# Decode step of attention and a gated MLP: the hidden vector as five neighbours a partition, w_out as the stationary operand

## The chip, the cores and the metric

The kernel runs on one core of a Trainium2 chip. The metric is the device time of one execution in microseconds; three runs of the kernel before gave 286.37, 286.49 and 287.57, with a median of 286.49. The profile is of a further execution, of 285.96 us, whose recorded span is 284.3 us. All times below inside the kernel count from the start of that span.

## What is computed

One token passes through one layer. The token x has D = 640 values. First, attention over the last 4096 keys of a cache of 32 heads with 192 values each; then a gated MLP of width 768. Cut to what matters:

```
q      = layernorm(x) @ wq                       # 640 -> 32 heads x 192
p      = softmax(q . k * 192**-0.5)              # over the last 4096 keys of each head
h      = x + (p . v) @ wo                        # 6144 -> 640
z      = gelu(layernorm(h) @ w_in)               # 640 -> 1536, halves z1 and z2
g      = w_sp * layernorm(z2) + b_sp             # one position: w_sp and b_sp are scalars
out    = h + (z1 * g) @ w_out                    # 768 -> 640, bf16
```

Nearly all bytes are keys and values: the page counts 119.34 MB read from memory.

## The kernel before

The work is a stream. All large loads go through one queue of SyncE in a fixed order, the list `plan`: wq, then keys `k_t` and values `v_t` of a pair of heads in turn (16 pairs), an eighth of wo (`wo_t`) after every second pair, and last the four pieces of w_in and the six of w_out. A load is issued when a buffer of its pool is free (`issue` and `free`): six for keys and values, two for wo. The schedule is written by hand (`manual_schedule`): each engine executes its instructions in the order in which the program text emits them.

For each pair, VectorE multiplies keys by the query (line 320), TensorE and ScalarE or VectorE add up the products (327, 310, 313), softmax follows with a maximum and `exps`, and TensorE multiplies by the values (`values`, 406 and 416). `scaled` and `columns`/`columns2` bring the result of a pair of pairs into columns, and `project` multiplies it by its eighth of wo:

- For the first seven eighths the result `o` is the stationary operand, one column wide, and rows of wo move. The sums lie in `rows`, a part of the PSUM bank `attn_ps`, in partitions 0 and 32 for the output columns up to `CUT[1]` = 384, and in 64 and 96 for the other 256 (line 477). x is added there as well (471).
- Then ScalarE copies `rows` to `rows_sb` (558), and `fold` (491) turns the rows into columns of `attn_ps` with three fp32 matmuls, each of 128 columns of `rows_sb` as the stationary operand against `halfsel`, which adds partitions 0 and 32, or 64 and 96. TensorE executes an fp32 matmul as two passes, so the profile shows six.
- For the last eighth a block of 128 columns of wo is the stationary operand and `o` moves (482), accumulating into the same columns. Its load comes in two halves, and each half of the projection has 15 matmuls.

So h lies in `attn_ps` as five columns of 128 partitions: value c x 128 + p in partition p, column c. From here on there is no more parallel work. Line 578 copies h to `h_pc` with its sum, 580 squares it, two matmuls with a matrix of 1/640 (582, 584) give the mean and mean square in every partition, and `ln_rstd16` (232 to 239) works out the reciprocal root on VectorE in five small instructions. `half_in` (593) does 30 matmuls with blocks of w_in as the stationary operand, first for z2, later for z1. After gelu (599), the second layernorm takes its sums by line 601 and the matmul 613; `gz` (622) is the gate, z1's gelu is line 625, and `gv` (627) their product.

The output of the MLP is formed as rows again. `orow` is a PSUM bank with four groups of 160 values, in partitions 0, 32, 64 and 96. `h_rows` writes h into it by 16 passes of fp32 matmuls against an identity, one half of them ahead of the matmul of line 613 and one half behind it. Then 24 matmuls with one column of `gv` as the stationary operand and 160 columns of w_out moving (630) add the MLP's output. VectorE casts the bank to bf16 (633), and the store writes four rows of 320 bytes (634).

Of the kernel before, what the change touches and what calls it, by code (L numbers as in the profile page):

```python
# [8 lines left out]
BF16 = mybir.dt.bfloat16  # L9
F32 = mybir.dt.float32  # L10
I32 = mybir.dt.int32
ALU = mybir.AluOpType
ACT = mybir.ActivationFunctionType
AX = mybir.AxisListType

@with_exitstack
def kernel(
# [14 lines left out]
    nc = tc.nc  # L32
    P = nc.NUM_PARTITIONS
    _, H, Sk, Dh = A_k_cache.shape
    D = A_x.shape[-1]
# [3 lines left out]
    DC = D // P  # L39
# [4 lines left out]
    FHC = Fh // P  # L44
# [23 lines left out]
    RQ = 4 * Dh // P  # L68
    NQ = NP // 2
    wo_v = A_wo.rearrange("(q e i) n -> q e (i n)", q=NQ, e=NE16)  # L70
    win_v = B_w_in.rearrange("(c p) f -> p c f", p=P)
    wout_v = B_w_out.rearrange("(c e i) n -> c e (i n)", c=FHC, e=NE16)
    wq_v = A_wq.rearrange("(c p i) n -> c p (i n)", c=DC, i=4)
    LAST = (0, J // 2, 3 * J // 4, 7 * J // 8, J)
# [8 lines left out]
    const = ctx.enter_context(tc.tile_pool(name="const", bufs=1))  # L83
    small = ctx.enter_context(tc.tile_pool(name="small", bufs=3))
    psum = ctx.enter_context(tc.tile_pool(name="psum", bufs=2, space=bass.MemoryType.PSUM))

    def sc_bank():
        return psum.tile([P, 512], F32, tag="sc", name="sc_ps", bufs=2)

    def bank():  # L90
        return psum.tile([P, 512], F32, tag="sm", name="sm_ps", bufs=3)
# [7 lines left out]
    w_out_sb = wp.tile([P, FHC, D], BF16)  # L99
# [51 lines left out]
    def free(kind, n=1):  # L151
        live[kind] -= n
        issue()
# [21 lines left out]
    ident_f = const.tile([P, P], F32)  # L175
# [8 lines left out]
    for a in range(2):  # L184
        nc.vector.tensor_reduce(out=par[:, a:a + 1], in_=ident_f[:].rearrange("p (g a s) -> p a g s", a=2, s=2)[:, a],
                                axis=AX.XY, op=ALU.add)
# [22 lines left out]
            nc.vector.tensor_reduce(out=blocks[:, h_, k_:k_ + 1], in_=id_h[:, c0:c0 + 2, :], axis=AX.XY, op=ALU.add)  # L209
    m8 = const.tile([P, 8], F32)  # L210
    nc.vector.tensor_tensor(out=m8[:], in0=blocks[:, 0, :], in1=blocks[:, 1, :], op=ALU.add)
    halfsel = const.tile([P, 2], F32)
    for h_ in range(2):
        nc.vector.tensor_reduce(out=halfsel[:, h_:h_ + 1], in_=ident_f[:, 64 * h_:64 * h_ + 64:32], axis=AX.X, op=ALU.add)
    pv_tiles = []
    for i in range(2):
        pv_tiles.append(psum.tile([P, 512], F32, name=f"pv{i}", bufs=1))
# [7 lines left out]
    def neg_var(mean, square):  # L225
        v = small.tile([P, 1], F32, tag="lnv", name="lnv")
        nc.vector.tensor_scalar(out=v[:], in0=mean, scalar1=mean, scalar2=square, op0=ALU.mult, op1=ALU.subtract)
        return v
# [25 lines left out]
    for a in range(2):  # L254
        nc.vector.tensor_scalar(out=xn2[:, :, a, :].rearrange("p c (g a s) -> p c a g s", a=2, s=2)[:, :, a],
                                in0=x_pc[:, 0, 0:DC, None, None].to_broadcast([P, DC, HALF // 2, 2]),
# [5 lines left out]
    for gq in range(0, NQ, 4):  # L262
        for w0 in range(0, 2 * Dh, P):
            psv = sc_bank()[:].rearrange("p (q w) -> p q w", q=4)
            for c in range(DC):
                wc = wq_sb[c // 2][:, (c % 2) * HD:(c % 2 + 1) * HD].rearrange("p (q a w) -> p q a w", q=NQ, a=2)
                for a in range(2):
                    nc.tensor.matmul(psv, lhsT=xn2[:, c, a, :], rhs=wc[:, gq:gq + 4, a, w0:w0 + P],  # L268
                                     start=(c == 0 and a == 0), stop=(c == DC - 1 and a == 1))
# [7 lines left out]
        nc.vector.tensor_scalar(out=sp_f[:, k_:k_ + 1], in0=sp_ps[:, c_:c_ + 1], scalar1=w_, scalar2=None, op0=ALU.mult)  # L277

    attn_ps = psum.tile([P, 512], F32, tag="acc", name="attn_ps", bufs=1)
    CUT = (0, 3 * P, D)  # L280
    rows = attn_ps[:, DC + 3:DC + 3 + CUT[1]]
    nc.vector.memset(rows, 0.0)
    nc.vector.memset(attn_ps[:, DC:DC + 1], (eps * DC) ** 0.5)
# [136 lines left out]
    def scaled(t):  # L420
        q, b = divmod(t, 2)
        if b == 0:
            obq[q] = small.tile([P, RQ, 2, 2, 32], BF16, tag="ob", name="ob", bufs=2)
        ob = obq[q][:, :, 0, b, :]
        pv = pv_tiles[t % 2]
        if t == NP - 1:
            pv1 = pv[:, 0:Dh].rearrange("p (r i) -> p i r", i=RQ)
            R2 = RQ // 2
            for k_ in range(2):
                o_last.append(small.tile([P, R2, 32], BF16, tag=f"ol{k_}", name=f"ol{k_}", bufs=1))  # L430
            nc.vector.tensor_copy(out=o_last[0][:], in_=pv1[:, 0:R2])
            nc.scalar.copy(out=o_last[1][:], in_=pv1[:, R2:])
            return
        o1 = small.tile([P, 8, 64], F32, tag="o1", name="o1", bufs=1)
        nc.vector.tensor_tensor(out=o1[:], in0=pv[:].rearrange("p (k w) -> p k w", k=8),
                                in1=m8[:, :, None].to_broadcast([P, 8, 64]), op=ALU.mult)
        flat = o1[:].rearrange("p k w -> p (k w)")
        for n, i0 in ((4, 0), (8, 4)):
            ni = 16 // n
            with nc.allow_low_precision(reason="one nonzero term"):  # L440
                nc.vector.tensor_reduce(out=ob[:, i0:i0 + ni], in_=flat.rearrange("p (k r i) -> p i r k", k=n, i=ni),  # L441
                                        axis=AX.X, op=ALU.add)
# [15 lines left out]
    def project(q, oT):  # L458
        wo_t = tiles.pop(("wo", q))
        o = small.tile([P, RQ], BF16, tag="o6", name="o6")  # L460
        rz = rzq.pop(q)
        if q < NQ - 1:
            o2v = oT[:, 0:2 * RQ].rearrange("p (i a) -> p a i", a=2)
            o0 = small.tile([P, RQ], F32, tag="o0", name="o0")
            nc.vector.tensor_scalar(out=o0[:], in0=o2v[:, 0], scalar1=rz[:, 0:1], scalar2=None, op0=ALU.mult)
            nc.vector.scalar_tensor_tensor(out=o[:], in0=o2v[:, 1], scalar=rz[:, 1:2], in1=o0[:], op0=ALU.mult, op1=ALU.add)
        else:
            nc.vector.tensor_scalar(out=o[:], in0=oT[:, 0:RQ], scalar1=rz[:, 0:1], scalar2=None, op0=ALU.mult)
        if q == 0:
            for h_ in range(2):  # L470
                nc.tensor.matmul(rows[64 * h_:64 * h_ + 1, 0:CUT[h_ + 1] - CUT[h_]], lhsT=ones_bf[0:1, 0:1],
                                 rhs=x_row[0:1, CUT[h_]:CUT[h_ + 1]], start=True, stop=False)
        for i in range(RQ):
            if q < NR:
                for h_ in range(2):
                    p0 = 32 * (i % 2) + 64 * h_
                    nc.tensor.matmul(rows[p0:p0 + 1, 0:CUT[h_ + 1] - CUT[h_]], lhsT=o[:, i:i + 1],  # L477
                                     rhs=wo_t[:, i * D + CUT[h_]:i * D + CUT[h_ + 1]],
                                     start=(q == 0 and i == 1), stop=(q == NR - 1 and i >= RQ - 2))
            else:  # L480
                for nb in range(DC):
                    nc.tensor.matmul(attn_ps[:, nb:nb + 1], lhsT=wo_t[:, i * D + nb * P:i * D + (nb + 1) * P],
                                     rhs=o[:, i:i + 1], start=False,
                                     stop=(q == NQ - 1 and i == RQ - 1 and nb == DC - 1))
        free("wo")

    def fold(rows_sb):
        n = CUT[1] // P
        for c in range(n):
            w = 2 if c + n < DC else 1  # L490
            nc.tensor.matmul(attn_ps[:, c:c + n * (w - 1) + 1:n], lhsT=rows_sb[:, c * P:(c + 1) * P], rhs=halfsel[:, 0:w],
                             start=(c == 0), stop=False)

    NR = NQ - 1
    assert NCH == 2
    for t in range(NP):
# [31 lines left out]
        if q_on:  # L528
            project((t - 5) // 2, oT)
# [24 lines left out]
    values(NP - 2, vt, J // 2, J)  # L554
    free("kv")
    project(NQ - 2, oT)
    rows_sb = const.tile([P, CUT[1]], F32)
    nc.scalar.copy(out=rows_sb[:], in_=rows)
    scaled(NP - 2)
    NG = 4  # L560
    OW = D // NG
    orow = sc_bank()[:, 0:OW]
    nc.vector.memset(orow, 0.0)
    vt = tiles.pop(("v", NP - 1))
    values(NP - 1, vt, 0, LAST[-3])
    fold(rows_sb)
    values(NP - 1, vt, LAST[-3], LAST[-2])
    oT = bank()
    columns(oT, NQ - 1, 0)
    values(NP - 1, vt, LAST[-2], J)  # L570
    scaled(NP - 1)
    columns(oT, NQ - 1, 1)
    project(NQ - 1, oT)

    h_pc = const.tile([P, DC], F32)
# [13 lines left out]
    def half_in(f0):  # L589
        zv = bank()  # L590
        for c in range(DC):
            for fb in range(FHC):
# [7 lines left out]
    tsq = small.tile([P, FHC + 1], F32, tag="tsq", name="tsq", bufs=1)  # L600
    nc.vector.scalar_tensor_tensor(out=tsq[:], in0=T3[:], scalar=1.0, in1=T3[:], op0=ALU.mult, op1=ALU.mult,
                                   accum_out=sums3[:, 1:2])
    def h_rows(g0, g1):
        for g in range(g0, g1):
            for c in range(DC):
                lo, hi = max(g * OW, c * P), min((g + 1) * OW, (c + 1) * P)
                if lo < hi:
                    nc.tensor.matmul(orow[32 * g:32 * g + 1, lo - g * OW:hi - g * OW], lhsT=h_pc[:, c:c + 1],
                                     rhs=ident_f[:, lo - c * P:hi - c * P], start=(lo == g * OW), stop=False)

    h_rows(0, NG // 2)
    lin_ps = bank()[:, 0:2]
    nc.tensor.matmul(lin_ps, lhsT=avgF_f[:], rhs=sums3[:], start=True, stop=True)
    h_rows(NG // 2, NG)
    v3 = neg_var(lin_ps[:, 0:1], lin_ps[:, 1:2])
    mw = small.tile([P, 1], F32, tag="mw", name="mw", bufs=1)
    nc.scalar.activation(out=mw[:], in_=lin_ps[:, 0:1], func=ACT.Copy, scale=sp_f[:, 2:3])
# [7 lines left out]
    nc.scalar.activation(out=z1[:], in_=z1_ps, func=ACT.Gelu_apprx_tanh, scale=rstd2)  # L625
    gv = small.tile([P, FHC], BF16, tag="gv", name="gv", bufs=1)
    nc.vector.tensor_tensor(out=gv[:], in0=z1[:], in1=gz[:], op=ALU.mult)
    for c in range(FHC):
        for g in range(NG):
            nc.tensor.matmul(orow[32 * g:32 * g + 1, :], lhsT=gv[:, c:c + 1], rhs=w_out_sb[:, c, g * OW:(g + 1) * OW],  # L630
                             start=False, stop=(c == FHC - 1))
    o_sb = small.tile([P, OW], BF16, tag="o_sb", name="o_sb", bufs=1)
    nc.vector.tensor_copy(out=o_sb[:], in_=orow)
    nc.sync.dma_start(out=out[0, 0].rearrange("(g n) -> g n", g=NG), in_=o_sb[0::32, :])

_INS = ['A_x', 'A_k_cache', 'A_v_cache', 'A_wq', 'A_wo', 'B_x', 'B_w_in', 'B_w_sp', 'B_b_sp', 'B_w_out']
_OUTS = [((1, 1, 640), 'bfloat16')]
# [24 lines left out]
```

## Time and profile before

| Stretch, us | What happens | TensorE clock granted |
|---|---|---|
| 266 to 268 | last values, seventh eighth of the projection | 0.51 |
| 268 to 272 | copy of rows, fold, values of the last pair | 1.00 |
| 272 to 274 | first half of the last eighth, wait for wo | 1.00 |
| 274 to 276 | h, its layernorm | 0.70 |
| 276 to 278 | z2 and the sums of its layernorm | 0.50 |
| 278 to 280 | gate, z1 | 0.50 |
| 280 to 282 | w_out, cast, issue of the store | 0.50 |
| 282 to 284.3 | store lands, end of the program | 0.50 |

| Instruction | Count | Mean, ns |
|---|---|---|
| weight load of line 482, 128x128 bf16 | 30 | 96 |
| weight load of line 593, 128x128 bf16 | 60 | 107 |
| weight load of line 491, 128x128 fp32 | 6 | 190 |
| matmul of line 630, 160 columns | 24 | 327 |
| cast of line 633, 128x160 | 1 | 323 |
| issue of the store, line 634 | 1 | 638 |

The mean of a weight load or a matmul is its length from start to end. They are pipelined: while one is under way the next has begun, so a group of 30 takes far less than thirty times that. What a group costs is read from the timeline, which gives start and length of the whole group. In the lists of the profile a line of a group shows the line of the program, the engine (PE is TensorE's matmul, PEld its weight load, DVE VectorE, ACT ScalarE, SPq the queue of SyncE), the operation and what it writes and reads; in brackets stands how long the engine had been idle ahead of it and what it waited for.

### The profile page before, as it was taken

Reading aid. Unit: us, or ns where it says so; the run is one execution under the profiler, and the core shown is the slowest. Engines: PE = TensorE matmul, PEld = TensorE weight load, DVE = VectorE, ACT = ScalarE, POOL = GpSimd, SP = SyncE. Lnnn points to the kernel's source line nnn. Section 1 sums busy time; section 2 is a strip of 40 time slices with the busy share of each in tenths; the row PEclk is TensorE's granted clock in tenths of the full one; section 3 lists DMA queues with packets and bytes.
Section 4 is the critical chain, followed back from the end, with each engine's and each line's share of the span. In section 5 each row is a group of like instructions: output and inputs, shape, how many; then the busy total and the mean of one; then the engine's idle time right before and its main releaser. Section 6 shows DMA issues by size and latency. Waiting matters only on the chain.

```text
span 284.3 us, 3101 instructions
## 1 busy us (share of the span) xinstructions
PE 167.4 (59%) x1110; PEld 65.5 (23%) x1110; DVE 218.2 (77%) x288; ACT 75.2 (26%) x380; POOL 2.3 (1%) x10
## 2 busy tenths in 40 slices
PE   0329935673855476735751573536971767784774
PEld 0103312220212122211220121102320222331463
DVE  7300099999999999998499989996699949995443
ACT  2001347414264440132334440143101010202301
POOL 3000000000000000000000000000000000000000
PEclk9999979996588757955799569955797797989785
DMA  8999999999999999999999999999999999999993
GB/s 332 443 443 443 415 409 430 428 446 436 443 443 410 422 415 444 428 471 431 415 436 422 430 436 439 418 453 422 424 422 457 443 443 384 436 436 418 405 406 145
DMA packets 5500, 119.53 MB, mean 421 GB/s; under 512 B 973, under 2 KB 2254, under 8 KB 2830
## 3 DMA queue, kind: packets, MB, share of 16 engines
q1 hardware_dynamic: 5480, 119.35, 97.8%
q8 instruction: 8, 0.13, 0.2%
q14 instruction: 6, 0.05, 0.0%
q10 hardware_dynamic: 6, 0.00, 0.0%
HBM read 119.34 MB, written 0.00 MB: 420 GB/s over the span
## 4 chain that ended last, share of the span: by engine, by line
DMA 42%; DVE 40%; PE 13%; issue 2%; SPq 1%; ACT 0%; DVEq 0%; ACTq 0%
DVE k_t L320 22%; DMA k_t<-in_A_k_cache_dram 21%; DMA v_t<-in_A_v_cache_dram 9%; DMA wq_t<-in_A_wq_dram 6%; DMA wo_t<-in_A_wo_dram 5%; PE sc_ps L268 5%; DVE S L313 5%; DVE ob L441 4%; DVE S L334 4%; PE sc_ps L327 3%; PE attn_ps L477 1%; SPq L58 1%; PE pv_174 L416 1%; PE sm_ps L344 1%; DVE gm L346 1%
## 5 line engine op out<-in xcount | busy, mean ns | idle before, releaser
L327 PE MATMUL sc_ps<-k_t,ident_bf 128*128 128x512 bf16 x282 | 88.0, 471 | 52.5 <-DVE k_t L320 52.5
L320 DVE TENSOR_TENSOR k_t<-k_t,q_205 128x6144 bf16<-128x6144 bf16 x32 | 107.1, 3350 | 13.8 <-DMA k_t<-in_A_k_cache_dram 13.8
L310 ACT ACTIVATE k_t<-k_t 128x192 bf16<-128x192 bf16 x144 | 49.9, 348 | 32.7 <-DVE k_t L320 32.7
L327 PEld LDWEIGHTS <-ident_bf 128*128 128x128 bf16 x282 | 30.7, 114 | 100.6 <-issue 66.0
L310 ACT ACTIVATION_READ_ACCUMULATOR k_t<-k_t 128x1 f32 x144 | 26.9, 187 | 0.0
L313 DVE TENSOR_REDUCE S<-k_t 128x16 f32<-128x3072 bf16 x8 | 26.8, 3344 | 0.0
L268 PE MATMUL sc_ps<-wq_t,xn_126 128*128 128x512 bf16 x60 | 17.4, 451 | 10.0 <-DMA wq_t<-in_A_wq_dram 7.8
L334 DVE TENSOR_REDUCE S<-sc_ps 128x16 f32<-128x512 f32 (+1 forms) x32 | 21.8, 681 | 0.0
L277 DVE TENSOR_SCALAR sp_f<-sm_ps 128x1 f32<-128x1 f32 x3 | 0.3, 151 | 24.9 <-PE sm_ps L274 24.9
L363 ACT ACTIVATE E_125<-S,bias 128x64 bf16<-128x64 f32 x10 | 3.5, 360 | 48.4 <-DVE bias L353 48.4
L363 ACT ACTIVATE E_123<-S,bias 128x64 bf16<-128x64 f32 x12 | 4.2, 360 | 42.2 <-DVE bias L353 42.2
L363 ACT ACTIVATE E_124<-S,bias 128x64 bf16<-128x64 f32 x10 | 3.5, 362 | 37.3 <-DVE bias L353 37.3
L270 ACT ACTIVATE q_205<-sc_ps 128x512 bf16<-128x512 f32 x6 | 3.6, 597 | 29.7 <-PE sc_ps L268 29.7
L268 PEld LDWEIGHTS <-xn_126 128*128 128x128 bf16 x60 | 6.5, 110 | 20.5 <-issue 13.1
L416 PE MATMUL pv_172<-v_t,E_125 128*8 128x512 bf16 (+1 forms) x72 | 8.2, 500 | 3.1 <-DMA v_t<-in_A_v_cache_dram 3.1
L346 DVE TENSOR_REDUCE gm<-sm_ps 2x1 f32<-2x128 f32 x16 | 4.5, 279 | 7.1 <-PE sm_ps L344 7.1
L416 PE MATMUL pv_174<-v_t,E_124 128*8 128x512 bf16 (+1 forms) x72 | 8.0, 488 | 1.9 <-DMA v_t<-in_A_v_cache_dram 1.9
L416 PE MATMUL pv_172<-v_t,E_123 128*8 128x512 bf16 (+1 forms) x72 | 6.2, 424 | 0.0
L416 PE MATMUL pv_174<-v_t,E_123 128*8 128x512 bf16 (+1 forms) x48 | 5.3, 490 | 1.3 <-DMA v_t<-in_A_v_cache_dram 1.3
L416 PE MATMUL pv_174<-v_t,E_125 128*8 128x512 bf16 (+1 forms) x48 | 5.0, 472 | 1.7 <-DMA v_t<-in_A_v_cache_dram 1.7
L416 PEld LDWEIGHTS <-E_125 128*8 128x8 bf16 (+1 forms) x120 | 3.5, 89 | 9.9 <-issue 8.1
L416 PEld LDWEIGHTS <-E_124 128*8 128x8 bf16 (+1 forms) x120 | 3.5, 87 | 7.6 <-issue 5.4
(237 smaller groups left out, 148.2 us busy)
## 6 DMA issues: line engine op xcount, KB each, us to landing
k_t<-in_A_k_cache_dram SPq DMA_DIRECT2D x15, 3072.0 KB, 29.8
v_t<-in_A_v_cache_dram SPq DMA_DIRECT2D x15, 3072.0 KB, 29.7
wq_t<-in_A_wq_dram SPq DMA_DIRECT2D x5, 1536.0 KB, 10.8
wo_t<-in_A_wo_dram SPq DMA_DIRECT2D x7, 960.0 KB, 20.0
k_t<-in_A_k_cache_dram SPq DMA_DIRECT2D x2, 1536.0 KB
v_t<-in_A_v_cache_dram SPq DMA_DIRECT2D x1, 1536.0 KB
w_in_sb<-in_B_w_in_dram SPq DMA_DIRECT2D x2, 576.0 KB, 14.6
wo_t<-in_A_wo_dram SPq DMA_DIRECT2D x2, 480.0 KB, 13.8
```

Source lines behind the costliest of these rows:

```text
L58: eng.add_instruction(mybir.InstDMACopy(name=nc.get_next_instruction_name(), mode="Copy", queue="qSPDynamicHW", ins=eng.lower_ap_dma(in_, ...
L268: nc.tensor.matmul(psv, lhsT=xn2[:, c, a, :], rhs=wc[:, gq:gq + 4, a, w0:w0 + P], start=(c == 0 and a == 0), stop=(c == DC - 1 and a == 1))
L270: nc.scalar.activation(out=q2f[:, gq:gq + 4, w0:w0 + P], in_=psv, func=ACT.Copy, scale=scale / 16)
L310: nc.scalar.activation(out=k3[:, j, :], in_=k3[:, j, :], func=ACT.Copy, accum_out=S[:, j:j + 1])
L313: nc.vector.tensor_reduce(out=st[t]["S"][:, J - JS:J], in_=products(t)[:, J - JS:J, :], axis=AX.X, op=ALU.add)
L320: nc.vector.tensor_tensor(out=kc, in0=kc, in1=q2[:, t:t + 1, :].to_broadcast([P, JC, Dh]), op=ALU.mult)
L327: nc.tensor.matmul(psv, lhsT=ident_bf[:], rhs=products(t)[:, j0:j1, n * g:(n + 1) * g], start=(n == 0), stop=(n == Dh // g - 1))
L334: nc.vector.tensor_reduce(out=S[:, j0:j1], in_=st[t]["ps"][ch], axis=AX.X, op=ALU.add)
L346: nc.vector.tensor_reduce(out=gm[:], in_=mT[0:2, 0:P], axis=AX.X, op=ALU.max)
L363: nc.scalar.activation(out=E[:, :, a], in_=S[:], func=ACT.Exp, bias=bias[:, a:a + 1], accum_out=zq[q][:, a, b:b + 1])
L416: nc.tensor.matmul(pv[p0:p0 + 2 * n, :].rearrange("p (k r i) -> p k r i", k=n, r=32), lhsT=E[:, j0:j0 + n, :].rearrange("p j a -> p (j a)" ...
L441: nc.vector.tensor_reduce(out=ob[:, i0:i0 + ni], in_=flat.rearrange("p (k r i) -> p i r k", k=n, i=ni), axis=AX.X, op=ALU.add)
```

## The change

The vector h is laid out differently: partition p holds the five neighbours 5p to 5p+4, one in each of the five columns, where it held p, 128+p, and so on. The output has the same layout, so each partition holds ten neighbouring bytes of it. This serves three purposes: h can be added to the MLP's output as it lies, without `h_rows`; w_out can be the stationary operand with `gv` moving, so that the output comes out as 128 partitions by 5; and the store has 128 equal rows.

What follows from it: w_in is read with (p c) in place of (c p), so that its rows meet the right values of h. The columns of wo in the last eighth, of `rows_sb` in the fold, and of w_out are taken with a step of five elements. The fold has five matmuls in place of three, from a `rows_sb` of 640 columns with zeros (a GpSimd memset in the setup) where a partition has nothing; `CUT` splits the columns in equal halves of 320, and ScalarE makes two copies of 64 partitions in place of one of 128. `orow`, its memset and `h_rows` are gone, and the cast becomes an addition of `h_pc`.

```diff
-    win_v = B_w_in.rearrange("(c p) f -> p c f", p=P)
+    win_v = B_w_in.rearrange("(p c) f -> p c f", p=P)
...
-    halfsel = const.tile([P, 2], F32)
-    for h_ in range(2):
-        nc.vector.tensor_reduce(out=halfsel[:, h_:h_ + 1], in_=ident_f[:, 64 * h_:64 * h_ + 64:32], axis=AX.X, op=ALU.add)
+    halfsel = const.tile([P, 1], F32)
+    nc.vector.tensor_reduce(out=halfsel[:], in_=ident_f[:, 0::32], axis=AX.X, op=ALU.add)
+    rows_sb = const.tile([P, D], F32)
+    nc.gpsimd.memset(rows_sb[:], 0.0)
...
-    CUT = (0, 3 * P, D)
+    CUT = (0, D // 2, D)
...
-                    nc.tensor.matmul(attn_ps[:, nb:nb + 1], lhsT=wo_t[:, i * D + nb * P:i * D + (nb + 1) * P],
+                    nc.tensor.matmul(attn_ps[:, nb:nb + 1], lhsT=wo_t[:, i * D + nb:(i + 1) * D:DC],
...
-    def fold(rows_sb):
-        n = CUT[1] // P
-        for c in range(n):
-            w = 2 if c + n < DC else 1
-            nc.tensor.matmul(attn_ps[:, c:c + n * (w - 1) + 1:n], lhsT=rows_sb[:, c * P:(c + 1) * P], rhs=halfsel[:, 0:w],
-                             start=(c == 0), stop=False)
+    def fold():
+        for c in range(DC):
+            nc.tensor.matmul(attn_ps[:, c:c + 1], lhsT=rows_sb[:, c::DC], rhs=halfsel[:], start=(c == 0), stop=False)
...
-    rows_sb = const.tile([P, CUT[1]], F32)
-    nc.scalar.copy(out=rows_sb[:], in_=rows)
+    for h_ in range(2):
+        nc.scalar.copy(out=rows_sb[64 * h_:64 * h_ + 64, CUT[h_]:CUT[h_ + 1]], in_=rows[64 * h_:64 * h_ + 64])
     scaled(NP - 2)
-    NG = 4
-    OW = D // NG
-    orow = sc_bank()[:, 0:OW]
-    nc.vector.memset(orow, 0.0)
...
-    def h_rows(g0, g1):
...
-    h_rows(0, NG // 2)
     lin_ps = bank()[:, 0:2]
     nc.tensor.matmul(lin_ps, lhsT=avgF_f[:], rhs=sums3[:], start=True, stop=True)
-    h_rows(NG // 2, NG)
...
+    o_ps = bank()[:, 0:DC]
     for c in range(FHC):
-        for g in range(NG):
-            nc.tensor.matmul(orow[32 * g:32 * g + 1, :], lhsT=gv[:, c:c + 1], rhs=w_out_sb[:, c, g * OW:(g + 1) * OW],
-                             start=False, stop=(c == FHC - 1))
-    o_sb = small.tile([P, OW], BF16, tag="o_sb", name="o_sb", bufs=1)
-    nc.vector.tensor_copy(out=o_sb[:], in_=orow)
-    nc.sync.dma_start(out=out[0, 0].rearrange("(g n) -> g n", g=NG), in_=o_sb[0::32, :])
+        for n in range(DC):
+            nc.tensor.matmul(o_ps[:, n:n + 1], lhsT=w_out_sb[:, c, n::DC], rhs=gv[:, c:c + 1],
+                             start=(c == 0 and n == 0), stop=(c == FHC - 1 and n == DC - 1))
+    o_sb = small.tile([P, DC], BF16, tag="o_sb", name="o_sb", bufs=1)
+    nc.vector.tensor_tensor(out=o_sb[:], in0=o_ps, in1=h_pc[:], op=ALU.add)
+    nc.sync.dma_start(out=out[0, 0].rearrange("(p n) -> p n", p=P), in_=o_sb[:])
```

## The prediction

> **What bounds the kernel now.** First I read the slice table of the page: is any engine or the memory stream full all the time, and until when?
>
> ```profile
> PEclk9999979996588757955799569955797797989785
> DMA  8999999999999999999999999999999999999993
> ...
> q1 hardware_dynamic: 5480, 119.35, 97.8%
> ```
>
> The transfers are busy in every slice but the last; the row of instruction totals gives VectorE 77%, TensorE 59%. So the stream of 119.35 MB sets the time until it ends, and only what comes after the last transfer that the result needs can be changed by work on the engines. The chain of waits, in order of time, says where that point lies:
>
> ```profile
> 259.82 13.82 DMA wo_t<-in_A_wo_dram
> 273.64 0.05 issue
> 273.69 0.54 PE attn_ps L482 x15
> ...
> 279.69 0.30 DVE gz L622
> ...
> 280.09 0.18 DVE gv L627
> ...
> 280.31 1.00 PE sc_ps L630 x14
> ...
> 281.33 0.32 DVE o_sb L633
> ```
>
> The first column is the start, the second the length. The last piece of wo lands at 273.64. Behind it lies a tail of 10.7 us to the end of the span (284.3): 15 matmuls that end the projection, the two layernorms, gelu, w_out, the evacuation and the store. From here on each step waits for the one before it, and the change edits this tail. The third reading is the timeline of TensorE shortly before, since the change also edits what stands in its queue there:
>
> ```profile
> 269.92 0.83 PE L491 MATMUL attn_ps<-halfsel,rows_sb 128*128 128x2 f32 x6
> 270.68 0.34 PE L406 MATMUL pv_174<-v_t,E_123 128*2 128x192 bf16 x8
> ...
> 271.36 0.34 PE L406 MATMUL pv_174<-v_t,E_123 128*2 128x192 bf16 x8 [0.22 <-DMA v_t<-in_A_v_cache_dram]
> ...
> 272.88 0.51 PE L482 MATMUL attn_ps<-o_1888,wo_t 128*128 128x1 bf16 x15 [0.32 <-DVE o_1888 L468]
> 273.69 0.53 PE L482 MATMUL attn_ps<-o_1888,wo_t 128*128 128x1 bf16 x15 [0.30 <-DMA wo_t<-in_A_wo_dram]
> ```
>
> TensorE reaches the second half of the last projection only 0.30 us ahead of its data. What delays the queue here by more than that moves the end.
>
> **What the Trainium skill says.** "TensorE: Matmul & The Clock Gate", section "Weight-path perf modes", has the fast weight load on for 128 columns of a type other than fp32, and reads them "packed or strided". The trace agrees for packed columns: 15 loads of wo_t with their matmuls take 0.51 us (34 ns each), 30 of w_in_sb 0.96 us (32 ns), while an fp32 pass of the fold takes 0.127 us (six from 269.92 to 270.68). No run here shows strided columns. "SBUF — State Buffer", section on the DMA port swizzle, says that a stride is free up to 8 bf16 or 4 fp32, since a 16-byte line has to be hit twice. A step of five is inside that for bf16 and outside for fp32. "DMA: Bandwidth & Descriptors", section "Why a DMA increments its semaphore by 16 and not by 1", says that the slowest dimension decides on how many engines a transfer runs: four rows on four engines, 128 on sixteen. The window of the store agrees: 8 packets in all, thus four of data and four of completion.
>
> **The change, part by part.**
>
> *w_in read as (p c).* The bytes and the runs (one half row of 1536 B per partition and chunk) stay as they are; only the DRAM rows that a partition takes change. The stream is full before and after: 0.
>
> *Setup.* One small reduction fewer and a GpSimd memset of 128x640; the wq transfers that the chain follows until 21.4 us hide both. The memset of rows is shorter by 64 columns on a VectorE stretch that the full stream hides too: 0.
>
> *CUT at 320.* The row-form projections pair pieces of 384 and 256 columns in separate column groups; the longer piece sets the time (0.69 us at full clock). Pieces of 320 make that some 0.1 us shorter. What waits is the release of a wo buffer, whose transfer queues behind a full stream: 0.
>
> *rows_sb.* One ScalarE copy of 128x384 (0.48 us from 268.53) becomes two of 64x320. Even at the old copy's length each they end at 269.49, ahead of 269.92 where the fold starts behind the matmuls that wait for v_t: 0.
>
> *The fold.* Three fp32 matmuls of two passes (six loads) become five (ten), and their columns lie 20 bytes apart. At 0.127 us a pass, the values matmuls behind the fold start at 269.92 + 10 x 0.127 = 271.19 in place of 270.68. Behind it are queued eight values matmuls and twelve columns matmuls, up to the last eight values matmuls (together some 0.40 us, estimated from 270.68 and 271.15, where the last of the columns matmuls ends), then the chain to the first half of the projection (271.36 to 272.88 = 1.52 us) and that half (0.51). The second half so starts at 271.19 + 2.43 = 273.62, just inside 273.69: nothing is lost at the packed price. If each pass doubles, the values matmuls start at 272.46 and the second half at 274.89: +1.20 us. The page gives the stride as too long but no price; I take one and a half, where the values matmuls start at 271.83 and the second half at 274.26: **+0.57 us**, ends 0 and +1.20.
>
> *The last projection with a step of five bf16.* Thirty loads at 10-byte steps. Lower end the packed 34 ns: 0. I take it, since the page counts five bf16 as free and the fast load as working with a step. The upper ends stand under the rivals.
>
> *h_rows removed.* The first eight of its sixteen matmuls run while VectorE works out rstd2 and end at 277.21, ahead of lin_ps at 277.58: 0. The second eight run 278.10 to 278.80 and hold back z1's thirty matmuls (278.74 to 279.70). Without them z1 is ready near 279.06, its gelu then follows Tw on ScalarE (279.22) and ends near 279.52 in place of 280.00. But gv waits as well for gz, which ends at 279.98 behind the rstd3 chain: gv starts at 280.03 in place of 280.09: **-0.06 us**. h is now added in the evacuation. The orow memset (0.19 us) lay in VectorE idle time: 0.
>
> *w_out.* 24 matmuls of 160 columns in four column groups, 0.97 us at the half clock that TensorE has there, become 30 loads of 128 columns with one moving column each. The same form over w_in_sb, at the same clock, took 0.96 us: **0**. The last w_out packets end near 280.4, and its six chunks are taken in order, the last at about 281.1: no new wait for data.
>
> *Evacuation.* A cast of 128x160 from PSUM, 0.32 us, becomes an addition of 128x5; the multiply of 128x6 that makes gv takes 0.17: **-0.15 us**.
>
> *The store.*
>
> ```profile
> 281.68 0.64 SPq L634 DMA_DIRECT2D out_dram<-o_sb  x1
> ```
>
> Four rows of 320 B become 128 of 10 B. A w_out transfer with 128 rows has a median issue of 0.47 us, so the issue may win 0.17. The packets: eight take 0.3% of 16 engines in a window of 2 us, about 12 ns each. An engine now has eight data packets and a completion one, some 0.1 us. Together **-0.1 us**; the writes of 10 B could cost what no transfer of this trace shows, and I keep +0.6 as the upper end.
>
> Sum: 0.57 - 0.06 - 0.15 - 0.1 = +0.26; 286.49 + 0.26 = **286.8 us**.
>
> **Rivals.**
>
> *No stride costs anything.* For it: the fold then ends 0.07 us ahead of what hides it. Against: 20 bytes is beyond the page's four fp32. -0.31 us: 286.2, **not slower**.
>
> *The strided bf16 load runs at half rate* (64 ns) and the fold doubles. For it: a 10-byte step touches 20 lines for 32 columns where packed columns touch 4. First half 0.96 us from 272.46 + 1.92 = 274.38, second from 275.34 (+1.65) and 0.45 longer than before; w_out +0.96; less 0.31: +2.75, **289.2**.
>
> *The fast load is lost.* At the fp32 pass's 0.127 us: halves of 1.90 us from 274.38 and 276.28 (+2.59, and 1.37 longer), w_out 3.81 in place of 0.97 (+2.84), less 0.31: +6.5, **293.0**. Against: the page allows steps up to 1024 elements.
>
> *The store is dear.* Ten-byte writes of 128 partitions into the same lines of memory have no row here. At +1.0 us for it in place of -0.1, on top of the forecast: **287.9**.
>
> A large gain has no place: the whole store from o_sb to the end of the span is 2.6 us of which most is issue, landing and shutdown that stay, and the other savings are 0.2 us.
>
> **How the numbers follow.** Forecast 0.42, free strides 0.22, half rate 0.17, lost fast load 0.09, dear store 0.10. Slower by over 0.5% is above 287.9: half rate, lost fast load, 0.06 of the dear store and 0.04 of the forecast (its fold at the upper end and a dearer store), 0.36. Faster by over 0.5% is below 285.06: no case reaches it by its sum, and I give it 0.08 of the free strides for a store or a chain that I have mis-sized. Same: 0.56. The range goes from 285.7 (free strides less 0.5) to 289.4 (half rate); the lost fast load, 0.07 below and 0.03 of half rate stay outside.
>
> **What would show it.** Ten fold passes from about 269.9: their spacing is 0.13, 0.19 or 0.25 us. Thirty loads of w_out_sb in about 1.0 us (fast), 2 (half) or 3.8 (lost). The start of the second half of the last projection: 273.7 if only the data hold it back, later if the fold does. An evacuation of 0.17 us. An issue of the store near 0.47 us, and the time from its end to the end of the span (1.9 us before). The prediction is wrong if the strided bf16 loads are spaced by over 50 ns, if the store takes over half a microsecond more, or if the wo landing itself moves.

## The result and the profile after

The changed kernel takes 289.7 us (median of six runs, 288.57 to 289.92), the kernel before 286.55 in the same comparison (286.15 to 287.57). The ratio is 1.0098, with a 95% interval of 1.0076 to 1.0121: slower by about 2.8 us; the two medians lie 3.15 us apart. The profiled executions have spans of 284.3 and 288.1 us, 3.88 us apart before rounding. That is more than the medians say, because the profiled execution of the changed kernel is the slowest of its six (289.92) and that of the kernel before, with 285.96, is faster than all six of its own. All of the 3.88 us can be found behind 264 us.

The slice table of the page, kernel after: the stream is as full and as large as before, and the span now has an empty slice at its end.

```profile
PEclk9999979797799558955777569865995989977755
DMA  8999999999999999999999999999999999999980
...
q1 hardware_dynamic: 5616, 119.35, 96.6%
```

The chain of waits of the kernel after, in order of time (start, length):

```profile
264.12 1.87 PE pv_173 L417 x12
...
270.88 2.29 PE attn_ps L490 x10
273.17 0.26 PE pv_175 L407 x6
...
274.95 1.34 PE attn_ps L483 x30
...
276.41 0.18 DVE h_pc L572 x2
...
282.28 0.18 DVE gv L611
...
282.60 1.35 PE sm_ps L615 x30
...
283.97 0.17 DVE o_sb L618
```

Before, the landing of wo stood in this chain, until 273.64; now it does not. From 264.12 on the chain runs through TensorE, past the fold (line 490, ten passes), and the thirty matmuls of the last projection (483) follow each other without a wait for data. The wait for memory has been replaced by work. Five stretches add up to the whole difference:

| Stretch | Before, us | After, us | Difference | Forecast |
|---|---|---|---|---|
| start to h_pc | 274.35 | 276.41 | +2.06 | +0.57 |
| h_pc to gv | 5.74 | 5.87 | +0.13 | -0.06 |
| gv to o_sb (w_out) | 1.24 | 1.69 | +0.45 | 0 |
| o_sb itself | 0.32 | 0.17 | -0.15 | -0.15 |
| end of o_sb to end of span | 2.60 | 4.00 | +1.40 | -0.1 |

Two further views bear on the first and the last row. The timeline of TensorE's stretch after:

```profile
268.81 2.07 PE L407 MATMUL pv_175<-v_t,E_123 128*2 128x192 bf16 x44
...
270.81 2.36 PE L490 MATMUL attn_ps<-halfsel,rows_sb 128*128 128x1 f32 x10
...
273.10 0.34 PE L407 MATMUL pv_175<-v_t,E_123 128*2 128x192 bf16 x8
...
274.95 1.32 PE L483 MATMUL attn_ps<-o_1889,wo_t 128*128 128x1 bf16 x30 [0.32 <-DVE o_1889 L469]
```

From 270.81 to 273.10 the ten passes take 0.229 us each, where the six before took 0.127. The clock isn't what makes them slow: over 270.80 to 273.10 alone it was 1.00. They also start 0.89 us later than before. The table of stretches (length; busy time of TensorE, its weight load, VectorE, ScalarE and GpSimd with counts; then granted clock, transfer share, GB/s) shows why for this execution: TensorE had the half clock until 270.4 and was busy throughout, while in the profile before it had the full one from 268.

```profile
268.00:270.00 2.00, 2.00 (x44) 1.18 (x36) 1.38 (x2) 0.60 (x2) 0.00 (x0) 0.50 0.95 387
270.00:272.00 2.00, 2.00 (x32) 1.75 (x22) 1.35 (x2) 0.24 (x1) 0.00 (x0) 0.90 1.01 411
```

SyncE's waits at the end, first after, then before (total, times, longest):

```profile
SPq L642 <- DMA out_dram<-o_sb: 2.5, 1, 2.5
```

```profile
SPq L657 <- DMA out_dram<-o_sb: 0.7, 1, 0.7
```

The issue of the store became shorter, 0.35 us in place of 0.64, and the wait for its completion longer, 2.5 in place of 0.7. The view of the transfers in the window from 285 to 286 us shows that the packets are not what takes the time:

```profile
DMA  1654442100000000000000000000000000000000
...
q1 hardware_dynamic: 144, 0.00, 7.7%
```

All 144 packets (128 rows and 16 completions) begin in the first eight of 40 slices, by 285.2. SyncE goes on at 287.0 (the issue's start at 284.16, plus 0.35 and 2.5). So 1.8 us pass with no packet on record. The Trainium skill, "DMA: Bandwidth & Descriptors", section "Anatomy of one DMA — SWDGE (gpsimd) path", attributes most of the fixed time of a transfer that GpSimd issues to the receipt of the last write, ahead of the semaphore. This store is issued by SyncE, and its trace has the time in the same place. Before, the packets end at 283.0 and the wait at the same 283.0, so four rows of 320 bytes had next to none of it.

### The profile page after: what moved, and what is told of

The parts are those of the page before. It is cut to its first block, busy times and chain, and to the rows that moved or that the text cites. A ratio compares the mean times of both kernels' runs of the same rounds, so it can differ in the third digit from the quotient of the medians.

```text
span 288.1 us, 3092 instructions
## 1 busy us (share of the span) xinstructions
PE 168.3 (58%) x1104; PEld 67.0 (23%) x1104; DVE 218.5 (76%) x286; ACT 75.5 (26%) x381; POOL 2.8 (1%) x11
## 4 chain that ended last, share of the span: by engine, by line
DVE 40%; DMA 37%; PE 18%; issue 2%; SPq 1%; ACT 0%; DVEq 0%; ACTq 0%
DVE k_t L321 21%; DMA k_t<-in_A_k_cache_dram 20%; DMA v_t<-in_A_v_cache_dram 10%; DMA wq_t<-in_A_wq_dram 6%; PE sc_ps L328 5%; DVE S L314 5%; PE sc_ps L269 4%; DVE ob L442 4%; DVE S L335 4%; PE pv_173 L417 2%; PE pv_175 L417 1%; PE attn_ps L478 1%; PE sm_ps L345 1%; PE attn_ps L490 1%; PE pv_175 L407 1%
## 5 line engine op out<-in xcount | busy, mean ns | idle before, releaser
L269 PE MATMUL sc_ps<-wq_t,xn_126 128*128 128x512 bf16 x60 | 16.7, 438 | 9.9 <-DMA wq_t<-in_A_wq_dram 7.7
L417 PE MATMUL pv_173<-v_t,E_125 128*8 128x512 bf16 (+1 forms) x72 | 7.9, 488 | 3.2 <-DMA v_t<-in_A_v_cache_dram 3.2
L417 PE MATMUL pv_175<-v_t,E_124 128*8 128x512 bf16 (+1 forms) x72 | 8.6, 517 | 0.5 <-DMA v_t<-in_A_v_cache_dram 0.5
L417 PE MATMUL pv_173<-v_t,E_123 128*8 128x512 bf16 (+1 forms) x72 | 6.5, 431 | 0.0
L417 PE MATMUL pv_175<-v_t,E_123 128*8 128x512 bf16 (+1 forms) x48 | 5.8, 521 | 0.7 <-DMA v_t<-in_A_v_cache_dram 0.7
L417 PE MATMUL pv_175<-v_t,E_125 128*8 128x512 bf16 (+1 forms) x48 | 5.0, 473 | 1.6 <-DMA v_t<-in_A_v_cache_dram 1.6
```

The source lines that it names most:

```text
L417: nc.tensor.matmul(pv[p0:p0 + 2 * n, :].rearrange("p (k r i) -> p k r i", k=n, r=32), lhsT=E[:, j0:j0 + n, :].rearrange("p j a -> p (j a)" ...
```

## The experiments

Three suspects remain: the fp32 fold with a step of five, the bf16 blocks with a step of five, and the completion of the store. Against them stood the clock as a rival, since the profile after had half the clock ahead of the fold. The clock ahead of the fold isn't the change's doing, though: of the five traces of the kernel before with only another last transfer, all have half the clock up to 270 or later, and their folds start at 270.73 to 271.33. Each suspect is taken out of the changed kernel alone, and all three together.

**The store taken out.**

```diff
-    nc.vector.tensor_tensor(out=o_sb[:], in0=o_ps, in1=h_pc[:], op=ALU.add)
-    nc.sync.dma_start(out=out[0, 0].rearrange("(p n) -> p n", p=P), in_=o_sb[:])
+    nc.vector.tensor_tensor(out=o_sb[:, 0:DC], in0=o_ps, in1=h_pc[:], op=ALU.add)   # o_sb: 160 wide, zeros
+    nc.sync.dma_start(out=out[0, 0].rearrange("(g n) -> g n", g=4), in_=o_sb[0::32, :])
```

> The kernel after, but its result of five columns is put into the first columns of a tile of zeros, and four rows of 320 bytes of that tile are stored, behind the same addition; so the output holds only 20 of the values of h. Theory that completion of the 128 rows of 10 bytes costs: from the end of o_sb to the end of the span 2.6 us as before in place of 3.96, SyncE's wait for the store 0.7 us in place of 2.5, and 1.3 to 1.4 us less than after: near 288.3. Rival, that the end of the program is longer for another reason: wait and time as after, 289.7.

Measured: 288.61 us, ratio to before 1.0079 (1.0064 to 1.0094). The wait is 0.7 us, as before, and from the end of o_sb (283.65) to the end of the span (286.2) pass 2.5 us. The stretch behaves as expected. The ratio moved by only 0.0019 against the change's 1.0098, some 0.5 us in place of 1.40; but the two intervals overlap, so these ratios leave the size of the gain open. A cleaner comparison follows below.

**The fold packed.**

```diff
-        nc.scalar.copy(out=rows_sb[64 * h_:64 * h_ + 64, CUT[h_]:CUT[h_ + 1]], in_=rows[64 * h_:64 * h_ + 64])
+        nc.scalar.copy(out=rows_sb[64 * h_:64 * h_ + 64].rearrange("p (c j) -> p c j", c=DC)[:, :, 64 * h_:64 * h_ + 64],
+                       in_=rows[64 * h_:64 * h_ + 64].rearrange("p (j c) -> p c j", c=DC))
...
-lhsT=rows_sb[:, c::DC]
+lhsT=rows_sb[:, c * P:(c + 1) * P]
```

> The kernel after, but ScalarE writes rows_sb in the order in which the fold reads it, so the five columns of the fold are packed; the result is the same. Theory that the step of five fp32 makes a pass slow: ten passes in 1.3 us in place of 2.3, h_pc 0.7 to 1.0 us earlier behind the fold, so near 288.8. Rival, that the fold is late only because TensorE had the half clock from 264 to 270 us in that profile: passes spaced as in after, time within 0.3 us of 289.7.

Measured: 287.61 us, ratio 1.0049 (1.0033 to 1.0065), so about 1.4 us less than the change by the ratios. The timeline of its TensorE:

```profile
270.41 1.28 PE L490 MATMUL attn_ps<-halfsel,rows_sb 128*128 128x1 f32 x10
271.62 0.34 PE L407 MATMUL pv<-v_t,E 128*2 128x192 bf16 x8
```

A pass takes 0.121 us, at full clock. ScalarE's two copies still take 0.85 us together. h_pc starts at 274.92, 1.49 us ahead of the change's: 0.40 because the fold starts earlier, which is not the edit's doing, and 1.08 because it is shorter. The expectation of 0.7 to 1.0 us for the edit was a little low.

**The bf16 blocks packed.**

```diff
-lhsT=wo_t[:, i * D + nb:(i + 1) * D:DC]
+lhsT=wo_t[:, i * D + nb * P:i * D + (nb + 1) * P]
...
-lhsT=w_out_sb[:, c, n::DC]
+lhsT=w_out_sb[:, c, n * P:(n + 1) * P]
```

> The kernel after, but the stationary blocks of wo in the last eighth and of w_out are packed columns, so values of h and of the output stand in a permuted order. Theory that a step of five bf16 makes a load 44 ns in place of 33: thirty loads of w_out_sb in 1.0 us in place of 1.33, thirty of wo_t likewise, in sum 0.5 to 0.7 us less than after: near 289.1. Rival, that w_out in 30 loads is slow for another reason (its first load not taken ahead, TensorE's clock): spacing stays 44 ns and the time 289.7.

Measured: 288.7 us, ratio 1.0080 (1.0065 to 1.0095). The timeline of the weight load, here and in the kernel after, for w_out:

```profile
282.04 0.89 PEld L615 LDWEIGHTS <-w_out_sb 128*128 128x128 bf16 x30 [1.48 <-issue]
```

```profile
282.57 1.28 PEld L615 LDWEIGHTS <-w_out_sb 128*128 128x128 bf16 x30 [1.49 <-issue]
```

Thirty loads take 0.89 us in place of 1.28: 30 ns against 43. The rival that the spacing has another reason is out, since clock (0.50) and order of the work are the same in both. The last projection's matmuls likewise take 0.94 in place of 1.32, also at 0.50 in both. The times by themselves do not show the gain: the interval of this ratio overlaps with that of the change. The stretches do, with 0.38 and 0.39 us.

**All three.**

> The three together: store of four rows, packed fold, packed wo and w_out (permuted values, 20 of them stored). If these three are the whole of the loss, the time is that of before less 0.1 to 0.3 us for the shorter evacuation: 286.2 to 286.6. If something else of the change costs (the new order of w_in's rows, the two copies, the lost row groups of w_out), over 287.2.

Measured: 286.22 us, ratio 1.0001 (0.9985 to 1.0016); h_pc starts at 274.52 and the span is 284.1. That is the time of the kernel before. The new order of w_in's rows, the two copies, the setup, w_out in thirty packed loads and the shorter evacuation therefore come to nothing in sum, within the interval of some 0.45 us either way. This kernel shows where the time is; it computes permuted values and stores few of them, so it is no version to use.

**Only the store left.** Fold and bf16 blocks packed, the store as in the change.

> The kernel after with packed fold and packed wo and w_out (values in permuted order), so that of the three costs only the store of 128 rows of 10 bytes is left. Theory that the three are the whole and add up: h_pc near 274.5, SyncE's wait for the store 2.1 to 2.5 us, and 1.1 to 1.4 us over the kernel with all three taken out (ratio 1.0001 to before), so 1.004 to 1.005. Rival, that with the others gone the store costs under 0.6 us, as the first comparison of times suggests: ratio under 1.002.

Measured: 287.8 us, ratio 1.0052 (1.0035 to 1.0069), SyncE's wait 2.2 us. Against all three the store costs 0.0051, or 1.5 us. This is near what the stretch in the profile says, and more than the 0.5 us of the first comparison. The sixteen times lie in two groups: twelve from 286.99 to 288.21, with a median of 287.6, 1.4 us above all three, and four from 289.23 to 289.70. These four have the lowest mean clock of the sixteen, 0.778. The profiled execution, with 289.5, is one of them, and its weight loads and stretch say what happened in it:

```profile
271.25 2.21 PEld L490 LDWEIGHTS attn_ps<-halfsel,rows_sb 128*128 128x128 f32 x10 [0.33 <-issue]
```

```profile
271.30:273.50 2.20, 2.20 (x16) 2.18 (x17) 0.17 (x1) 0.00 (x0) 0.00 (x0) 0.50 1.02 402
```

The columns of this fold are packed, and still a pass takes 0.221 us: the granted clock was 0.50. h_pc started at 276.72, where I expected 274.5. So the clock, the rival of the second experiment, is real as well. A pass took 0.229 us with a step at full clock, and 0.221 packed at half clock. The packed bf16 loads did not change with the clock: the thirty matmuls of the last projection take 0.94 us here, at 0.50, and 0.94 in the kernel with all three taken out, at 1.00.

**The store alone, in the kernel before.**

```diff
-    nc.sync.dma_start(out=out[0, 0].rearrange("(g n) -> g n", g=NG), in_=o_sb[0::32, :])
+    nc.sync.dma_start(out=out[0, 0].rearrange("(g n) -> g n", g=128), in_=o_sb[0:128, 0:5])
```

> The kernel before, but its last transfer takes five columns of each of 128 partitions and stores 128 rows of 10 bytes (the output holds the first five of each group's values and zeros). Theory that these rows are slow to complete: SyncE's wait for the store 2.1 to 2.5 us in place of 0.7, its issue 0.35 in place of 0.64, so 1.1 to 1.4 us over before: near 287.6. Rival, that the wait is long after the change only through its addition or its other layout: 286.0 to 286.4, a little shorter by the issue.

Measured: 287.76 us, ratio 1.0044 (1.0031 to 1.0058), which is 1.3 us; wait 2.2 us, issue 0.35 us. The store costs as much without anything else of the change. By the stretches the six traces with neighbouring rows of 10 bytes have 3.55 to 4.00 us from the end of o_sb to the end of the span, and the three with four rows of 320 bytes 2.52 to 2.60, so the profile after lies at the upper end.

**When the store completes late.** Four kernels, each the kernel before with another last transfer, each traced once. Three of them write to a scratch area and store zeros to the output early; only the wait of SyncE is read from them.

```diff
+    scratch = nc.dram_tensor("scratch_dram", (128, 512), BF16, kind="Internal").ap()
+    nc.sync.dma_start(out=scratch[0:128, 0:32], in_=o_sb[0:128, 0:32])
```

> The kernel before, but zeros are stored to the output early, and the last transfer takes 32 columns of each of 128 partitions into 128 rows of 64 bytes of a scratch area, 1024 bytes apart. Theory that it is the short rows that complete late: wait of SyncE for this store near 0.7 us less what the quicker issue leaves over, thus up to 1.2. Rival, that it is the number of rows or of the sixteen completions: 2.1 us or more.

With rows of 10 bytes in the same places (0:5 in place of 0:32):

> As the one before, but rows of 10 bytes, 1024 bytes apart, so that no two rows lie close together. Theory that each short row costs by itself: wait 2.1 to 2.5 us as with the change. Rival, that rows wait for each other because several lie in the same piece of memory: 0.7 to 1.2 us.

With a scratch area of (128, 5), so that these rows follow each other:

> As the store of 128 rows of 10 bytes to the scratch area, but the rows follow each other without a gap, as in the output. Theory that short rows wait for each other where several lie in the same piece of memory: SyncE's wait 2.1 to 2.5 us, where rows 1024 bytes apart had 0.9. Rival, that the scratch area completes faster than the output whatever the rows: 0.9 us.

And 80 rows of 16 bytes to the output (g=80, o_sb[0:80, 0:8]):

> The kernel before with a store of 80 rows of 16 bytes (16 engines as with 128 rows; values in other places, zeros). If the wait grows with the number of neighbouring rows in one piece of memory (taken as 64 bytes, four rows in place of 6.4): 0.9 + 1.3 x 3/5.4 = 1.6 us. If what costs is a row that isn't a multiple of some small unit, 16 bytes would be free: 0.9.

| Last transfer | Issue, us | SyncE's wait, us |
|---|---|---|
| before: 4 rows of 320 B, neighbours | 0.64 | 0.7 |
| 128 rows of 64 B, 1024 B apart | 0.33 | 0.9 |
| 128 rows of 10 B, 1024 B apart | 0.33 | 0.9 |
| 80 rows of 16 B, neighbours | 0.37 | 0.7 |
| 128 rows of 10 B, neighbours, scratch | 0.33 | 2.1 |
| 128 rows of 10 B, neighbours, output | 0.35 | 2.2 |

It is not the number of rows, not their shortness alone, and not the output's place in memory. Rows of 10 bytes were slow to complete only as neighbours, in six traces with waits of 2.1 to 2.5 us. My measure for that, pieces of 64 bytes, is wrong: 16-byte rows lie four to such a piece, and I expected 1.6 us for them, yet they complete in 0.7. What stays open is whether it counts that two rows of 10 bytes share a piece of 16 bytes or less, or that most of them do not start at a multiple of 16 bytes. The rows 1024 bytes apart avoid both, and no run here separates the two. Nor was a store of 128 neighbouring rows of 16 bytes tried, so whether 128 neighbours in place of 80 matter is open too.

**The price of a step.** Groups of matmuls with one moving column ahead of the query projection, each group with another step between the stationary columns.

```diff
+    for kw in loads(zt, 5, 16, ones_bf[:, 0:1]):      # zt[:, 0:127 * 5 + 1:5] as lhsT, 16 times
+        nc.tensor.matmul(st_ps[:, 0:1], **kw)         # one such pair of lines for each step
```

> The kernel before, and ahead of its query projection groups of 16 bf16 and 8 fp32 matmuls of one moving column, each group with another step between the 128 columns of its stationary block: bf16 steps 1, 2, 3, 4, 5, 6, 8, 10 and fp32 steps 1 to 5. Only the spacing inside each group is of use. Theory of lines of 16 bytes: bf16 spacing about 32 ns up to step 2 or 4, 44 at 5, growing up to step 8 to twice and then flat; fp32 pass 0.12 us at step 1 and 2, 0.23 at 4 and 5. Rival, that any step but one loses the fast load: bf16 over 100 ns or at once 44 from step 2 on, fp32 0.23 from step 2 on.

The timeline of the weight load; each line is a group of 16, and the distance of two starts over 16 is the price of one load:

```profile
9.76 0.50 PEld L267 LDWEIGHTS <-xn 128*128 128x128 bf16 x16 [2.35 <-DVE xn L255]
10.18 0.50 PEld L269 LDWEIGHTS <-xn 128*128 128x128 bf16 x16
10.61 0.53 PEld L271 LDWEIGHTS <-xn 128*128 128x128 bf16 x16
11.06 0.61 PEld L273 LDWEIGHTS <-xn 128*128 128x128 bf16 x16
11.58 0.72 PEld L275 LDWEIGHTS <-xn 128*128 128x128 bf16 x16
12.21 0.84 PEld L277 LDWEIGHTS <-xn 128*128 128x128 bf16 x16
12.95 1.07 PEld L279 LDWEIGHTS <-xn 128*128 128x128 bf16 x16
13.92 1.07 PEld L281 LDWEIGHTS <-xn 128*128 128x128 bf16 x16
14.88 3.52 PEld L283 LDWEIGHTS sm_ps<-ones_f,xn 128*128 128x128 f32 x16
```

bf16 with steps of 1, 2, 3, 4, 5, 6, 8 and 10: 26, 27, 28, 33, 39, 46, 61 and 60 ns. The price rises slowly up to 3, then by 5 to 8 ns a step, and from 8 to 10 no more; that is the shape that the theory gave. In the kernel, packed and at a step of five, it was some 4 ns more. The rival, that a step loses the fast load at once, is out. The fp32 groups, all at 0.21 to 0.23 us a pass, said nothing of the step. What clock they had isn't on record: the table of stretches prints 1.00, but the first entry of the clock in this trace begins at 36.7 us, behind all groups. A second run put them behind the query projection:

> The kernel before, and behind its query projection, where TensorE has been busy and has the full clock, groups of 8 fp32 matmuls (16 passes) with a step of 1, 2, 3, 4, 5 between the stationary columns. In the run ahead of the projection all steps took 0.21 us a pass, step 1 too, at what looks like half the clock. Theory that at full clock a pass is bound by the reads and doubles with the step: 0.12 us at step 1, 0.23 at 5, and the step at which it leaves 0.12 shows how much is free. Rival, that the clock alone matters: all steps alike, 0.12.

```profile
34.76 1.84 PE L280 MATMUL sm_ps<-ones_f,xn 128*128 128x1 f32 x16
36.46 2.02 PE L282 MATMUL sm_ps<-ones_f,xn 128*128 128x1 f32 x16
38.34 3.44 PE L284 MATMUL sm_ps<-ones_f,xn 128*128 128x1 f32 x16
41.64 3.85 PE L286 MATMUL sm_ps<-ones_f,xn 128*128 128x1 f32 x16
```

Step 1 takes 0.106 us a pass, step 2 0.118. During the third group, at 38.87, the clock fell to 0.50, and from there on each step takes 0.21 to 0.23. The first four loads of the third group start ahead of that, at 38.32, 38.48, 38.66 and 38.83: step 3 takes 0.17 us at full clock. So the pass does get slower with the step at full clock, as the theory said, and at half clock the steps are nearly alike. Step 4 at full clock stays open. Step 5 at full clock is known from the fold of the kernel with the store of four rows: 2.28 us for ten passes, with a clock of 1.00 from 268 to 274.

## Why the prediction was right and where it was wrong

The direction was right, the size was not: 286.8 us forecast, 289.7 measured, which lies 0.3 above the range. The ratio of 1.0098 on the time of 286.49 gives 289.3, at its upper end. The likeliest case was the wrong one. The half-rate rival has nearly the measured time (289.2), but by luck: its doubled fold came close, its doubled bf16 load was too dear, its cheap store too cheap, and these two errors pull in opposite directions. One of the signs that the prediction set for being wrong was met: the store took over half a microsecond more.

- *The bound.* This is right: the stream did not change, and all of the difference lies in the tail. It begins at 264, though, where the two timelines are still 0.1 us apart, and not at the fold.
- *The fold.* The mechanism is right, but the term was mis-sized. I took one and a half times the packed price; at full clock it is 1.8 (0.229 against 0.127). I also took 269.92 as a fixed start. It depends on the clock that TensorE has while it works through the values ahead (270.81 in the profile after), and with the full clock from 268 on the landing of v_t, for which TensorE waited in two others (270.33 and 270.41). In the kernel before, the slack ahead of wo absorbs most of such a delay: with other last transfers, three of its traces have the fold at 270.73 to 270.85 and h_pc only 0.15 to 0.30 us later than the profile before. In the two where half the clock lasted into the fold (271.27 and 271.33) h_pc is 0.96 and 1.59 later. With ten slow passes nothing is left to absorb a delay.
- *The last projection and w_out, "Lower end the packed 34 ns: 0. I take it".* This step failed. The load costs 43 ns with the step and 30 to 34 without. On w_out that is 0.35 us, and gv to the first matmul takes 0.1 more. On the last projection it is 0.38, once the fold has used up the slack. The ground for it was the sentence of the Trainium skill, "SBUF — State Buffer", section on the DMA port swizzle, that a bf16 stride up to eight is free; the table of steps shows otherwise, and the measurement decides. That the fast load works with a step is confirmed: 39 ns at step 5 is far from the 127 ns that I gave a lost one.
- *h_rows, w_in, the setup, CUT, the copies.* These are right, in sum: the kernel with the three costs taken out has the ratio 1.0001. The 0.06 us that I gave to an earlier z1 did not come. gv follows gz by the same 0.1 us as before, so gz alone was the limit.
- *The evacuation.* This is right, with -0.15 us.
- *The store, "Together -0.1 us".* This step failed most. The issue did shorten (by 0.29 us), and the packets were as quick as estimated. What I left out was the time between the last packet and the completion. I had noted that no row of the trace shows such writes, bounded it at +0.6, and gave a rival with +1.0 a chance of 0.10. The whole stretch measured +1.40 in the profile, and 1.3 and 1.5 us by the ratios of the two experiments that isolate the store.

By the profiles the terms are 2.06 + 0.13 + 0.45 - 0.15 + 1.40 = 3.89 us, the 3.88 of the spans but for rounding. The 0.13 comes from the two layernorm sums (0.59 us for the first in place of 0.40), at a clock of 0.50 where the stretch had 0.70 on average. Of the 2.06, part is the clock of that execution too: the kernel with the store of four rows has the same fold and last projection, and its h_pc, with the full clock from 268, starts 0.49 us earlier (275.93).

No experiment points to a version that beats the kernel before. The packed fold, which computes what the change computes, improves it to 1.0049 but leaves the store and the bf16 step.

## What to carry to other kernels

A layout that makes one instruction simpler has to be priced at every place that reads or writes it; here the output's ten bytes a partition cost some 1.4 us and the stepped stationary blocks the rest, while the work removed was hidden already. When a wait for memory is followed at once by a queue on one engine, ask how much slack that queue has, and whether it still has it when the engine's clock is half. For a transfer of a form that the trace of the kernel before doesn't have, measure issue, packets and completion apart: here completion, with 1.8 us, was the largest of the three.

## What the runs showed that I had not expected

- 128 neighbouring rows of 10 bytes complete 1.8 us after their last packet, while the same rows 1024 bytes apart, or 80 neighbouring rows of 16 bytes, make SyncE wait 0.9 and 0.7 us in all.
- A packed fp32 pass of 128 columns took 0.11 to 0.13 us at full clock and 0.22 at half; thirty packed bf16 loads took the same 0.94 us at both. The step of five slows the fp32 pass at full clock to 0.229, but at half clock a packed pass is as slow. The passes ahead of the query projection, of 0.21 us, are at a clock that isn't on record.
- The price of a stepped bf16 load grows gradually: 26 ns packed, 28 at a step of three, 33 at four, 61 at eight, and 60 at ten.
